# Sums of exponentials by products with ones instead of GpSimd additions, in a fused attention and mixture kernel

## The chip, the cores and the metric

The kernel runs on one core of a Trainium2 chip. The metric is the time of one execution in microseconds (us), measured on the device; several runs are made and the median counts. A core has five engines that run side by side and wait for one another by semaphores: TensorE (PE in the rows; its weight loads are PEld), VectorE (DVE), ScalarE (ACT), GpSimd (POOL) and SyncE (SP), which issues the DMAs.

## What is computed

Three layers, one behind the other. The change is in the first, an attention over pooled queries:

```python
q_pool = q.reshape(B, H, S // 2, 2, D).mean(axis=3)        # B, H, S, D = 4, 8, 1152, 64
scores = np.matmul(q_pool, k.transpose(0, 1, 3, 2)) / np.sqrt(D)
attn = np.exp(scores - scores.max(-1, keepdims=True))
attn = attn / (attn.sum(-1, keepdims=True) + 1e-09)
x = np.matmul(attn, v)                                     # 576 queries a head, 1152 keys
```

Then x (2304 x 512) goes through a soft mixture of eight experts (logits against `phi`, a softmax over the tokens, two products an expert, a softmax over the slots), and its output through a last layer with `w_in` and `w_out` and a piecewise quadratic function between them. `w_in` and `w_out` arrive as 64-bit floats and are turned into 32-bit ones by integer operations on VectorE.

## The kernel before

The attention works on 16 pairs of heads, P = 0 to 15. A pair has nine steps c = 0 to 8 of 128 keys, and each step has two half-steps h (one a head). One loop over g = 9P + c writes the order of all engines by hand. In half-step (c, h) of pair P it puts, in this order:

- `max_half` (line 308): four products into a score tile `mx` for a pair that is 11 steps ahead, whose maximum VectorE takes at line 320 (`mp`). Four such steps give the maxima that are subtracted from the scores later;
- `st` (line 374): eight products into a score tile `st`, and on ScalarE the exponential `e` (line 379), a tile of 128 keys x 576 queries in 32-bit floats;
- `pv` (line 395) of the step before: the products of `e` with the values into `acc[P, i]`, one PSUM bank for each half i of the 576 queries, 288 columns of 512 used;
- whatever `plan` and a table of cast steps have put into the slot (g, h) with `at`.

`mx`, `st` and the small tiles of the tail share a pool of three score tiles. So the products `st` of a half-step need the tile whose maximum VectorE took in the half-step before, or wait for it.

The divisors of the softmax are the sums of `e` over the 1152 keys. In the kernel before, GpSimd adds the nine `e` of each head up (`es_first`, line 389, and `es_add`, line 385); the first addition of the second head is on VectorE, and so are all additions of the last pair. `tail_sum` (line 410, `ts`), in step 10 of the pair, that is step 1 of the next one, sums over the 128 partitions by four products with a column of ones, each into 32 partitions of a score tile, and ScalarE copies the result to `sq` (line 412). The transposes `tr` (line 423), `tx` (434) and `tb` (461) and the division follow in steps 11 to 13.

VectorE has other work in the slots: the cast of `w_out` and `w_in` (lines 190 to 214, tile `wst`, 11 of the 18 half-steps of a pair, from the end of pair 0 to pair 13), `kn` (line 263) and `qn` (286) that prepare keys and queries of a later pair, and `mm` and `qn` (353, 355) that close the maxima. After the maxima of a pair are closed, a DMA transposes `qn` into `q`, which `st` of that pair reads. GpSimd also adds the query pairs (line 276, one instruction a pair).

The attention ends at about 552 us of the span; experts and last layer follow, and the change does not touch them.

Of the kernel before, what the change touches and what calls it, by code (L numbers as in the profile page):

```python
# [33 lines left out]
LQK = 20  # L34
LPT = 6
WPH = 3
ESF = 0, 1
ESE = (lambda n: n.gpsimd, lambda n: n.vector)
REA = 0


@with_exitstack
def fused_kernel(ctx: ExitStack, tc: tile.TileContext, q, k, v, phi, w1, w2, w_in, w_out, out):
    nc = tc.nc
# [12 lines left out]
    LEAD = NK + 2  # L57
# [27 lines left out]
    zcol = cols[0:128, 1:2]  # L85
# [7 lines left out]
    ones = cols[0:128, 10:11]  # L93
# [71 lines left out]
    xT = x_p.tile([128, HPB, TQ], F32, tag="xT", name="xT")  # L165
# [193 lines left out]
    E, Es, acc = {}, {}, {}  # L359

    def acc_tile(i, name):
        return acc_p.tile([128, 512], F32, tag=f"acc{i}", name=name)
# [16 lines left out]
        nc.scalar.activation(out=e, in_=ps[:, :, 0:HQ], func=AF.Exp, scale=ESC)  # L379
        E[P, c, h] = e  # L380

    def es_add(P, c, h):

        eng = nc.vector if P == NP - 1 or h == 1 and NK * P + c >= NP * NK - LEAD else nc.gpsimd
        eng.tensor_tensor(out=Es[P, h], in0=Es[P, h], in1=E[P, c, h], op=ALU.add)  # L385

    def es_first(P, h):
        Es[P, h] = g3.tile([128, 2, HQ], F32, tag=f"es{h}", name=f"es{P}_{h}")
        (nc.vector if P == NP - 1 else ESE[h](nc)).tensor_tensor(out=Es[P, h], in0=E[P, 0, h], in1=E[P, 1, h], op=ALU.add)

    def pv(P, c, i):
        if c == 0:
            acc[P, i] = acc_tile(i, f"acc{P}_{i}")
        for h in range(2):
            nc.tensor.matmul(acc[P, i][h * 64:(h + 1) * 64, 0:HQ], lhsT=vt[P][:, h, c, :], rhs=E[P, c, h][:, i, :],  # L395
                             start=(c == 0), stop=(c == NK - 1))


    xr, ss = {}, {}
# [2 lines left out]
        xr[P] = xT[:, P % HPB, :]  # L402
        nc.scalar.activation(out=xr[P][:, i * HQ:(i + 1) * HQ], in_=acc[P, i][:, 0:HQ], func=AF.Copy)

    def tail_sum(P):
        ps = sc_tile(f"ts{P}")
        for h in range(2):
            for i in range(2):
                j = 2 * h + i
                nc.tensor.matmul(ps[32 * j:32 * j + 32, 0, 0:HQ], lhsT=ones.to_broadcast([128, 32]), rhs=Es[P, h][:, i, :], start=True, stop=True)  # L410
        sq = xT[:, 1, 0:HQ] if P == NP - 1 else Es[P, 0][:, 0, :] if P == NP - 2 else g2.tile([128, HQ], F32, tag="sq", name=f"sq{P}")
        nc.scalar.activation(out=sq, in_=ps[:, 0, 0:HQ], func=AF.Copy)
        xr[P, "s"] = sq

    def tail_fin(P, src):
        ss[P] = g4.tile([TT, 3, 4], F32, tag="ss", name=f"ss{P}")
# [154 lines left out]
        for _ in range(n):  # L571
            nc.tensor.matmul(bt["warm"][0][:, 0:128], lhsT=ident, rhs=ident, start=True, stop=True)

    sched = {}

    def at(g, slot, f, *a):
        sched.setdefault((g, slot), []).append((f, a))

    def plan(P):
        b = NK * P  # L580
        if P > 1:
            at(b - LQK, 0, load_qk, P)
            for h in range(2):
                at(b - 18, h, prep_khi, P, h)
                at(b - 17, h, prep_klo, P, h)
                at(b - 17, h, xpose_k, P, h)
            at(b - 18, 0, prep_qp, P)
            at(b - 16, 0, prep_qhi, P)
            at(b - 16, 0, xpose_q1, P)
            at(b - 15, 0, prep_qlo, P)  # L590
            at(b - 15, 1, dup_q1, P)
        if P > 0:
            at(b - 8, 1, load_v, P)
            at(b - 9 if P > 1 else 1, 1, s2_fill, P)
        for h in range(2):
            at(b + 2, ESF[h], es_first, P, h)
            at(b + 9, h, tail_raw, P, h)
        for c in range(2, NK):
            for h in range(2):
                at(b + c, 1, es_add, P, c, h)  # L600
        at(b + 10, 0, tail_sum, P)
        last = P == NP - 1
        if not last:
            at(b + 11, REA, tail_rec, P)
        for i in range(2):
            at(b + (10 if last else 12), i if last else TXN[i], tail_xn, P, i)
            if last:
                at(b + 12, i, tail_mul, P, i)
        if not last:
            for c, sl, *a in TMUL:  # L610
                at(b + c, sl, tail_mul, P, *a)
        if last:
            at(b + 11, 0, tail_rec, P)
        at(b + 13, 1, tail_xt, P)
        if P % HPB == HPB - 1:
            q_ = P // HPB
            if last:
                at(b + LPT, 1, lg_part, q_)
# [26 lines left out]
    with tc.manual_schedule():  # L645
# [6 lines left out]
        for i in range(2):  # L652
            eng = nc.gpsimd if i else nc.vector
# [39 lines left out]
        for g in range(-LEAD, nsteps + 1):  # L693
            mx = [divmod(g + LEAD, NK)] if not NK <= g + LEAD < 2 * NK else []
            mx += [(1, t) for t in range(NK) if P1G[t] == g]
            P, c = divmod(g, NK)
            for h in range(2):
                for PM, tm in mx:
                    if PM < NP:
                        max_half(PM, tm, h)  # L700
                        if h == 1 and tm == NK - 1:
                            max_fin(PM)
                if 0 <= g < nsteps:
                    st(P, c, h)
                if g >= 1:
                    pv(*divmod(g - 1, NK), h)
                slot(g, h)
            if g >= 27 and g % 9 == WPH and nloaded < NWA:
                w_load()
            for ends, gx, nw, nm in ((nsteps - 24, g0x, NW0, "w0"), (nsteps - 19, g1x, NW1, "w1"), (nsteps - 9, g2x, NW2, "w2"),  # L710
                                    (nsteps, gkx, NWK, "wk")):
                if g == ends:
                    gx.close()
                    pool = wtop.enter_context(tc.tile_pool(name=nm, bufs=1, side="right"))
                    wslot += [pool] * nw
                    for _ in range(nw):
                        w_load()
# [33 lines left out]
        ps = over_slots(sc_tile("sT")[:, 0, :], Prun)  # L751
        n = 4 * NS + 4
# [353 lines left out]
```

## Time and profile before

| what | value |
|---|---|
| median of three runs | 817.34 us (816.13 to 818.74) |
| the profiled execution: its time | 819.79 us |
| the profiled execution: its span, first to last instruction | 818.0 us |
| busy in the span: PE / DVE / ACT / POOL | 89% / 78% / 53% / 58% |
| the chain that ended last, by engine | PE 52%, DVE 36%, DMA 5%, issue 4% |
| its largest line | DVE `mp` L320, 13% |

The busy share of TensorE counts an instruction from its start to its modelled end, and products overlap, so it reads too high: how long a product holds the engine is read from the distance of the starts in the timeline. A group's row gives the busy time, the mean of one in ns, and the idle time ahead of it with the engine that ended it. A row of waits gives the sum, how many, and the longest.

### The profile page before, as it was taken

Reading aid. Unit: us, or ns where it says so; the run is one execution under the profiler, and the core shown is the slowest. Engines: PE = TensorE matmul, PEld = TensorE weight load, DVE = VectorE, ACT = ScalarE, POOL = GpSimd, SP = SyncE. Lnnn points to the kernel's source line nnn. Section 1 sums busy time; section 2 is a strip of 40 time slices with the busy share of each in tenths; the row PEclk is TensorE's granted clock in tenths of the full one; section 3 lists DMA queues with packets and bytes.
Section 4 is the critical chain, followed back from the end, with each engine's and each line's share of the span. In section 5 each row is a group of like instructions: output and inputs, shape, how many; then the busy total and the mean of one; then the engine's idle time right before and its main releaser. Section 6 shows DMA issues by size and latency. Waiting matters only on the chain.

```text
span 818.0 us, 17073 instructions
## 1 busy us (share of the span) xinstructions
PE 731.4 (89%) x6744; PEld 534.7 (65%) x6744; DVE 635.1 (78%) x816; ACT 435.9 (53%) x807; POOL 477.3 (58%) x327
## 2 busy tenths in 40 slices
PE   7888888799787888978879989899999999999998
PEld 6665566566565565655656667563378888888887
DVE  6989999998999998999999886445176787666620
ACT  4345556465564564645646556540166767565530
POOL 7397688775877877667777697100234554434330
PEclk9999999999999999999999999999999999999999
DMA  9967859687797598885978862689990000000000
GB/s 207 224 131 178 195 112 238 196 224 172 196 229 202 171 212 219 212 209 144 225 218 202 195 170 88 208 296 347 392 367 28 27 13 14 26 26 26 26 27 26
DMA packets 144096, 135.37 MB, mean 165 GB/s; under 512 B 80912, under 2 KB 100624, under 8 KB 143632
## 3 DMA queue, kind: packets, MB, share of 16 engines
q1 hardware_dynamic: 144016, 134.28, 60.2%
q8 instruction: 53, 0.87, 0.4%
q14 instruction: 27, 0.22, 0.1%
HBM read 91.29 MB, written 17.30 MB: 133 GB/s over the span
## 4 chain that ended last, share of the span: by engine, by line
PE 52%; DVE 36%; DMA 5%; issue 4%; ACT 1%; SPq 1%; DVEq 0%; ACTq 0%
DVE mp L320 13%; PE st L374 8%; PE po L1009 8%; PE po L1008 8%; PE po L1010 8%; PE acc L395 7%; DVE wst L191 4%; PE mx L308 4%; DVE wst L190 3%; DVE wst L199 3%; DVE wst L196 2%; DVE qn L286 2%; PE h L945 2%; PE h L761 2%; DVE qn L355 2%
## 5 line engine op out<-in xcount | busy, mean ns | idle before, releaser
L385 POOL TENSOR_TENSOR es<-es,e 128x576 f32<-128x576 f32 x208 | 323.0, 1576 | 82.7 <-ACT e L379 71.3
L379 ACT ACTIVATE e<-st 128x576 f32<-128x576 f32 x288 | 187.1, 650 | 192.4 <-PE st L374 185.5
L320 DVE TENSOR_REDUCE mp<-mx 128x1 f32<-128x576 f32 x282 | 209.1, 748 | 29.7 <-PE mx L308 29.2
L395 PE MATMUL acc<-e,vf 128*64 128x288 f32 x1152 | 200.2, 412 | 0.3 <-ACT e L379 0.3
L374 PE MATMUL st<-q,K 128*64 128x288 f16 x1152 | 126.3, 290 | 55.2 <-DVE mp L320 53.0
L308 PE MATMUL mx<-K,q 128*64 128x288 f16 x1152 | 127.7, 294 | 18.9 <-DVE mp L320 15.4
L964 POOL TENSOR_TENSOR glo<-r,ghi 128x1024 fp32r<-128x1024 f32 x34 | 81.7, 2404 | 101.5 <-ACT ghi L963 101.5
L374 PE MATMUL st<-q,S 128*64 128x288 f16 x1152 | 126.8, 289 | 2.6 <-DMA q<-qn 2.6
L374 PEld LDWEIGHTS <-K 128*64 128x64 f16 x1152 | 72.1, 110 | 80.1 <-issue 73.8
L308 PEld LDWEIGHTS <-q 128*64 128x64 f16 x1152 | 70.2, 111 | 78.6 <-issue 43.5
L958 DVE TENSOR_TENSOR r<-cl,r 128x1024 f32<-128x1024 f32 x34 | 81.2, 2388 | 38.6 <-ACT cl L957 38.6
L1008 PE MATMUL po<-whi,ghi 128*128 128x512 f32 (+1 forms) x280 | 107.6, 384 | 0.0
L1009 PE MATMUL po<-wlo,ghi 128*128 128x512 f32 (+1 forms) x280 | 107.6, 384 | 0.0
L1010 PE MATMUL po<-whi,glo 128*128 128x512 f32 (+1 forms) x280 | 107.2, 383 | 0.0
L395 PEld LDWEIGHTS acc<-e,vf 128*64 128x64 f32 x1152 | 85.3, 139 | 3.3 <-ACT e L379 1.5
L374 PEld LDWEIGHTS <-S 128*64 128x64 f16 x1152 | 73.8, 111 | 5.1 <-issue 3.1
L948 ACT ACTIVATE r<-h,cols 128x512 f32<-128x512 f32 x68 | 42.9, 686 | 32.9 <-PE h L945 31.4
L1010 PEld LDWEIGHTS po<-whi,glo 128*128 128x128 f32 x280 | 52.6, 188 | 10.5
L1008 PEld LDWEIGHTS po<-whi,ghi 128*128 128x128 f32 x280 | 52.7, 188 | 9.6
L1009 PEld LDWEIGHTS po<-wlo,ghi 128*128 128x128 f32 x280 | 52.7, 188 | 9.3
L949 DVE TENSOR_SCALAR cl<-h 128x512 f32<-128x512 f32 x68 | 43.7, 686 | 18.1 <-ACT r L948 16.7
L963 ACT ACTIVATE ghi<-r 128x1024 fp32r<-128x1024 f32 x34 | 36.1, 1062 | 19.2 <-DVE r L958 19.1
(191 smaller groups left out, 877.9 us busy)
## 6 DMA issues: line engine op xcount, KB each, us to landing
w<-in_moe_w_dram SPq DMA_DIRECT2D x31, 1024.0 KB, 7.8
vf<-in_v_dram SPq DMA_DIRECT2D x16, 576.0 KB, 5.1
kf<-in_k_dram SPq DMA_DIRECT2D x30, 288.0 KB, 3.8
f<-in_moe_w_out_dram SPq DMA_DIRECT2D x16, 512.0 KB, 4.3
f<-in_moe_w_in_dram SPq DMA_DIRECT2D x16, 512.0 KB, 5.6
qf<-in_q_dram SPq DMA_DIRECT2D x30, 256.0 KB, 4.4
S<-K SPq DMA_DIRECT2D x16, 288.0 KB, 5.8
out_dram<-ob SPq DMA_DIRECT2D x17, 256.0 KB, 2.0
```

What stands on the lines that cost most here:

```text
L308: nc.tensor.matmul(ps[p0:p1, i, 0:HQ], lhsT=q1[P][:, t, p0:p1], rhs=kk[:, j * HQ:(j + 1) * HQ], start=True, stop=True)
L320: nc.vector.tensor_reduce(out=mp[P][:, t, a:a + 1], in_=ps[:, :, 0:HQ], op=ALU.max, axis=AX.XY)
L374: nc.tensor.matmul(ps[c0:c0 + 64, i, 0:HQ], lhsT=kk[:, ci, c0:c0 + 64], rhs=f[:, sl[i]], start=first, stop=not first)
L379: nc.scalar.activation(out=e, in_=ps[:, :, 0:HQ], func=AF.Exp, scale=ESC)
L385: eng.tensor_tensor(out=Es[P, h], in0=Es[P, h], in1=E[P, c, h], op=ALU.add)
L395: nc.tensor.matmul(acc[P, i][h * 64:(h + 1) * 64, 0:HQ], lhsT=vt[P][:, h, c, :], rhs=E[P, c, h][:, i, :], start=(c == 0), stop=(c == NK - 1))
L949: nc.vector.tensor_scalar(out=cl[:, a:b], in0=src, scalar1=-1.0, scalar2=1.0, op0=ALU.max, op1=ALU.min)
L958: nc.vector.tensor_tensor(out=r[:, sl], in0=cl[:, sl], in1=r[:, sl], op=ALU.add)
L964: nc.gpsimd.tensor_tensor(out=glo[n, qd][:, sl], in0=r[:, sl], in1=ghi[n, qd][:, sl].bitcast(F32), op=ALU.subtract)
L1008: nc.tensor.matmul(po, lhsT=ghi[n, qd][:, j, sl], rhs=whi[:, f, cs], start=(f == 0), stop=False)
L1009: nc.tensor.matmul(po, lhsT=ghi[n, qd][:, j, sl], rhs=wlo[:, f, cs], start=False, stop=False)
L1010: nc.tensor.matmul(po, lhsT=glo[n, qd][:, j, sl], rhs=whi[:, f, cs], start=False, stop=(f == 15))
```

## The change

VectorE now adds pairs of steps alone: (0, 1), (2, 3) and (4, 5), six additions a pair of heads, one step after the second `e` (`GRP`; `es_add`, line 387 of the new file). Steps 6, 7 and 8 are not added at all. GpSimd adds nothing. The six groups (three sums and three single `e`) go to TensorE: `es_sum` (line 397 of the new file) multiplies each with the column of ones, for the four combinations j of head and query half, each into 32 partitions. The result is accumulated in the banks of the values behind the 288 columns in use: 192 query columns into `acc[P, 0]`, the other 96 into `acc[P, 1]`. The table `TAT` says where: group 0 in half-step (3, 1), group 1 in (5, 1), groups 2 and 3 in (7, 1), and groups 4 and 5 in (0, 0) of the next pair, each time between `st` and `pv`.

Since the two uses of a bank start at different times, both are started by products of zeros, two a bank, over 480 and 384 columns (in `pv` for c = 0, line 407 of the new file), and the other products only add. `tail_sum` issues no products any more: ScalarE copies the 192 and 96 columns to `sq` in half-steps (0, 0) and (0, 1) of the next pair, right behind `tail_raw`. The score tile `ts` is gone.

```diff
+GRP = ((0, 1), (2, 3), (4, 5), (6,), (7,), (8,))
+TAT = ((3, 1, (0,)), (5, 1, (1,)), (7, 1, (2, 3)), (9, 0, (4, 5)))
...
-        eng = nc.vector if P == NP - 1 or h == 1 and NK * P + c >= NP * NK - LEAD else nc.gpsimd
-        eng.tensor_tensor(out=Es[P, h], in0=Es[P, h], in1=E[P, c, h], op=ALU.add)
...
+    def es_sum(P, ns):
+        for n in ns:
+            for i, (c0, c1) in enumerate(((0, 192), (192, HQ))):
+                for j in range(4):
+                    h = j // 2
+                    src = Es[P, n, h] if len(GRP[n]) > 1 else E[P, GRP[n][0], h]
+                    nc.tensor.matmul(acc[P, i][32 * j:32 * j + 32, HQ:HQ + c1 - c0], lhsT=ones.to_broadcast([128, 32]),
+                                     rhs=src[:, j % 2, c0:c1], start=False, stop=False)
...
+            n = HQ + (192 if i == 0 else HQ - 192)
+            z = ident.bitcast(F16)[:, 0:n // 2].unsqueeze(1).to_broadcast([128, 2, n // 2])
+            for h in range(2):
+                nc.tensor.matmul(acc[P, i][h * 64:(h + 1) * 64, 0:n].rearrange("p (a b) -> p a b", a=2),
+                                 lhsT=zcol.bitcast(F16)[:, 0:1].to_broadcast([128, 64]), rhs=z, start=True, stop=False)
...
-                             start=(c == 0), stop=(c == NK - 1))
+                             start=False, stop=(c == NK - 1))
...
-    def tail_sum(P):
-        ps = sc_tile(f"ts{P}")
...
+        c0, c1 = (0, 192) if i == 0 else (192, HQ)
+        nc.scalar.activation(out=xr[P, "s"][:, c0:c1], in_=acc[P, i][:, HQ:HQ + c1 - c0], func=AF.Copy)
...
-            at(b + 2, ESF[h], es_first, P, h)
+            for n, cs in enumerate(GRP):
+                for c in cs[1:]:
+                    at(b + c + 1, h, es_add, P, n, h, c)
             at(b + 9, h, tail_raw, P, h)
-        for c in range(2, NK):
-            for h in range(2):
-                at(b + c, 1, es_add, P, c, h)
-        at(b + 10, 0, tail_sum, P)
+            at(b + 9, h, tail_sum, P, h)
+        for c, i, ns in TAT:
+            pre[b + c, i] = P, ns
...
+                if (g, h) in pre:
+                    es_sum(*pre[g, h])
```

How the order moves is shown at three places. The first is VectorE in steps 4 and 5 of pair 7, before (`mp` is the maximum, `wst` the cast):

```order
L320 TENSOR_REDUCE mp_3502<-mx_6_0_3817 128x1 [waits PE_49]
L199 SCALAR_TENSOR_TENSOR wst_3645<-f_14_3408,wst_3645 128x512 [waits DVE_49]
L320 TENSOR_REDUCE mp_3502<-mx_6_1_3845 128x1 [waits PE_49]
L214 TENSOR_TENSOR wst_3645<-wst_3645,whi_3841 128x512 [waits Activation_49]
L320 TENSOR_REDUCE mp_3502<-mx_7_0_3877 128x1 [waits PE_49]
L190 TENSOR_SCALAR wst_3896<-f_15_3574 128x512 [waits DMAHW6_49,DMAHW4_49]
L191 TENSOR_SCALAR wst_3896<-wst_3896 128x512 [waits DVE_49]
```

And the same place in the changed kernel (its lines stand one further down):

```order
L321 TENSOR_REDUCE mp_3772<-mx_6_0_4119 128x1 [waits PE_49]
L387 TENSOR_TENSOR es_1_0_4142<-e_2_0_4016,e_3_0_4068 128x576 [waits Activation_49]
L200 SCALAR_TENSOR_TENSOR wst_3946<-f_14_3670,wst_3946 128x512 [waits DVE_49]
L321 TENSOR_REDUCE mp_3772<-mx_6_1_4149 128x1 [waits PE_49]
L387 TENSOR_TENSOR es_1_1_4176<-e_2_1_4047,e_3_1_4096 128x576 [waits Activation_49]
L215 TENSOR_TENSOR wst_3946<-wst_3946,whi_4145 128x512 [waits Activation_49]
L321 TENSOR_REDUCE mp_3772<-mx_7_0_4181 128x1 [waits PE_49]
L191 TENSOR_SCALAR wst_4200<-f_15_3858 128x512 [waits DMAHW6_49,DMAHW4_49]
L192 TENSOR_SCALAR wst_4200<-wst_4200 128x512 [waits DVE_49]
```

An addition stands ahead of the cast step in two half-steps that had the cast alone, and the next maximum stands behind both.

The second place is TensorE in half-step (1, 0) of pair 7, before, where the sums of pair 6 are taken behind the first value products of pair 7:

```order
L395 MATMUL acc_0_3665<-e_0_0_3615,vf_3234 64x288 [waits Activation_49]
L395 MATMUL acc_0_3665<-e_0_1_3638,vf_3234 64x288 [waits Activation_49]
L410 MATMUL ts_3668<-es_0_3264,cols 32x288 [waits PE_49,Pool_49]
L410 MATMUL ts_3668<-es_0_3264,cols 32x288
L410 MATMUL ts_3668<-es_1_3288,cols 32x288 [waits Pool_49]
L410 MATMUL ts_3668<-es_1_3288,cols 32x288
```

In the changed kernel the last two groups of pair 6 stand one step earlier, in half-step (0, 0) of pair 7, ahead of the value products of step 8 (`cols` holds the column of ones; `x2` are two rows that differ in the query half):

```order
L397 MATMUL acc_0_3457<-e_7_0_3788,cols 32x192 x2
L397 MATMUL acc_0_3457<-e_7_1_3816,cols 32x192 x2
L397 MATMUL acc_1_3485<-e_7_0_3788,cols 32x96 x2
L397 MATMUL acc_1_3485<-e_7_1_3816,cols 32x96 x2
L397 MATMUL acc_0_3457<-e_8_0_3851,cols 32x192 x2
L397 MATMUL acc_0_3457<-e_8_1_3875,cols 32x192 [waits Activation_49]
L397 MATMUL acc_0_3457<-e_8_1_3875,cols 32x192
L397 MATMUL acc_1_3485<-e_8_0_3851,cols 32x96 x2
L397 MATMUL acc_1_3485<-e_8_1_3875,cols 32x96 x2
L410 MATMUL acc_0_3457<-e_8_0_3851,vf_2981 64x288
```

Sixteen products stand where there were none, and the value products of the step come behind them.

The third place is TensorE at (1, 0) of pair 7 in the changed kernel, the same place as the second fence shows of before:

```order
L407 LDWEIGHTS cols
L407 MATMUL acc_0_3966<-ident,cols 64x480 [waits Activation_49]
L407 LDWEIGHTS cols
L407 MATMUL acc_0_3966<-ident,cols 64x480
L410 MATMUL acc_0_3966<-e_0_0_3897,vf_3490 64x288
L410 MATMUL acc_0_3966<-e_0_1_3938,vf_3490 64x288 [waits Activation_49]
```

The four products `ts`, with their two waits for GpSimd, are gone, and two products of zeros stand ahead of the value products, behind a wait for ScalarE's copies out of the bank.

## Rows read from the trace of the kernel before

**Rows 1.** Windows: start:end, us, busy of PE, PEld, DVE, ACT, POOL; clock, DMA, GB/s.

```profile
61.47:493.10 431.63, 366.17 (x4194) 256.61 (x4193) 405.13 (x524) 244.15 (x513) 324.29 (x207) 0.99 0.78 197
489.04:513.24 24.20, 24.20 (x295) 17.83 (x291) 15.37 (x20) 15.60 (x35) 18.70 (x15) 1.00 0.29 83
```

**Rows 2.** Waits of the whole span: engine, line, releaser, sum in us, times, longest.

```profile
PE st L374 <- DVE mp L320: 53.0, 57, 2.1
PE mx L308 <- DVE mp L320: 15.4, 23, 1.7
```

**Rows 3.** Groups by line and shape, VectorE, 61.47 to 493.10 us.

```profile
L320 DVE TENSOR_REDUCE mp<-mx 128x1 f32<-128x576 f32 x235 | 174.5, 748 | 15.7 <-PE mx L308 15.2
L191 DVE TENSOR_SCALAR wst<-wst 128x512 f32<-128x512 f32 x31 | 37.2, 1200 | 1.1
...
L389 DVE TENSOR_TENSOR es<-e,e 128x576 f32<-128x576 f32 x13 | 10.7, 823 | 0.0
L353 DVE TENSOR_TENSOR mm<-mp 128x9 f32<-128x9 f32 x13 | 5.2, 396 | 0.4
```

**Rows 4.** Instructions of one line, whole span: min/median/max ns, first and last start.

```profile
L191 DVE TENSOR_SCALAR wst<-wst x32: 426/1511/1558, 46.9 to 475.9; 128x512 f32<-128x512 f32 x32
L353 DVE TENSOR_TENSOR mm<-mp x16: 166/582/1055, 25.8 to 509.4; 128x9 f32<-128x9 f32 x15, 128x3 f32<-128x3 f32 x1
L385 DVE TENSOR_TENSOR es<-es,e x16: 751/759/1882, 511.9 to 541.1; 128x576 f32<-128x576 f32 x16
```

**Rows 5.** Timeline of VectorE and GpSimd at 475 us: start, us, engine, line.

```profile
475.51 3.13 POOL L385 TENSOR_TENSOR es<-es,e 128x576 f32<-128x576 f32 x2
475.86 1.52 DVE L191 TENSOR_SCALAR wst<-wst 128x512 f32<-128x512 f32 x1
...
477.30 0.74 DVE L320 TENSOR_REDUCE mp<-mx 128x1 f32<-128x576 f32 x1
```

**Rows 6.** Timeline of TensorE in two half-steps without a wait.

```profile
67.25 0.41 PE L374 MATMUL st<-q,K 128*64 128x288 f16 x4
...
67.73 0.65 PE L395 MATMUL acc<-e,vf 128*64 128x288 f32 x4
68.22 0.41 PE L308 MATMUL mx<-K,q 128*64 128x288 f16 x4
68.47 0.41 PE L374 MATMUL st<-q,K 128*64 128x288 f16 x4
...
69.54 0.53 PE L434 MATMUL tx<-ident,xT 128*96 128x128 f32 x3
...
70.27 0.41 PE L374 MATMUL st<-q,K 128*64 128x288 f16 x4
```

**Rows 7.** Timeline of TensorE around one call of the old sums.

```profile
60.60 0.94 PE L395 MATMUL acc<-e,vf 128*64 128x288 f32 x4
61.47 0.69 PE L410 MATMUL ts<-es,cols 128*32 128x288 f32 x8
62.09 0.44 PE L308 MATMUL mx<-K,q 128*64 128x288 f16 x4
```

**Rows 8.** Weight loads of the old sums: min/median/max ns.

```profile
L410 PEld LDWEIGHTS ts<-es,cols x128: 105/107/109, 61.5 to 542.3; 128*32 128x32 f32 x128
```

**Rows 9.** Groups of TensorE in 61.47 to 493.10 us: first and last of five for the logits.

```profile
L477 PE MATMUL lp<-xT,phs 128*32 128x288 f32 x48 | 3.5, 412 | 0.0
...
L524 PE MATMUL ln<-ident,xT 32*96 32x32 f32 x18 | 1.4, 210 | 0.9 <-ACT xT L513 0.9
```

**Rows 10.** Timeline of all engines where the last maxima close.

```profile
509.37 1.05 DVE L353 TENSOR_TENSOR mm<-mp 128x9 f32<-128x9 f32 x1
...
510.46 1.36 DVE L355 TENSOR_SCALAR qn<-mm 128x9 f16<-128x9 f32 x1
...
511.84 1.32 SPq L357 DMA_TRANSPOSE q<-qn  x1
...
513.24 0.50 PE L374 MATMUL st<-q,K 128*64 128x288 f16 x4
...
516.35 0.69 PE L374 MATMUL st<-q,S 128*64 128x288 f16 x4 [2.61 <-DMA q<-qn]
```

More of the change, by code (lines that the diff above doesn't have):

```diff
@@ L380, in st, with es_add @@
         E[P, c, h] = e
-    def es_add(P, c, h):
-        eng = nc.vector if P == NP - 1 or h == 1 and NK * P + c >= NP * NK - LEAD else nc.gpsimd
-        eng.tensor_tensor(out=Es[P, h], in0=Es[P, h], in1=E[P, c, h], op=ALU.add)
-    def es_first(P, h):
-        Es[P, h] = g3.tile([128, 2, HQ], F32, tag=f"es{h}", name=f"es{P}_{h}")
-        (nc.vector if P == NP - 1 else ESE[h](nc)).tensor_tensor(out=Es[P, h], in0=E[P, 0, h], in1=E[P, 1, h], op=ALU.add)
+    def es_add(P, n, h, c):
+        a, b = (E[P, GRP[n][0], h], E[P, c, h]) if c == GRP[n][1] else (Es[P, n, h], E[P, c, h])
+        if c == GRP[n][1]:
+            Es[P, n, h] = g3.tile([128, 2, HQ], F32, tag=f"es{h}", name=f"es{P}_{n}_{h}")
+        nc.vector.tensor_tensor(out=Es[P, n, h], in0=a, in1=b, op=ALU.add)
+    def es_sum(P, ns):
[6 more added lines that the diff above has]
+                                     rhs=src[:, j % 2, c0:c1], start=False, stop=False)
     def pv(P, c, i):
@@ L403, in tail_raw, with tail_sum @@
         nc.scalar.activation(out=xr[P][:, i * HQ:(i + 1) * HQ], in_=acc[P, i][:, 0:HQ], func=AF.Copy)
-    def tail_sum(P):
-        ps = sc_tile(f"ts{P}")
-        for h in range(2):
[L408 to L413, printed above, removed]
+    def tail_sum(P, i):
+        if i == 0:
+            last = [Es[x] for x in Es if x[0] == P and x[2] == 0][-1]
+            xr[P, "s"] = xT[:, 1, 0:HQ] if P == NP - 1 else last[:, 0, :] if P == NP - 2 else \
+                g2.tile([128, HQ], F32, tag="sq", name=f"sq{P}")
+        c0, c1 = (0, 192) if i == 0 else (192, HQ)
+        nc.scalar.activation(out=xr[P, "s"][:, c0:c1], in_=acc[P, i][:, HQ:HQ + c1 - c0], func=AF.Copy)
     def tail_fin(P, src):
@@ L572, in warm @@
             nc.tensor.matmul(bt["warm"][0][:, 0:128], lhsT=ident, rhs=ident, start=True, stop=True)
-    sched = {}
+    sched, pre = {}, {}
     def at(g, slot, f, *a):
@@ L595, in plan @@
         for h in range(2):
-            at(b + 2, ESF[h], es_first, P, h)
+            for n, cs in enumerate(GRP):
+                for c in cs[1:]:
+                    at(b + c + 1, h, es_add, P, n, h, c)
             at(b + 9, h, tail_raw, P, h)
-        for c in range(2, NK):
-            for h in range(2):
-                at(b + c, 1, es_add, P, c, h)
-        at(b + 10, 0, tail_sum, P)
+            at(b + 9, h, tail_sum, P, h)
+        for c, i, ns in TAT:
+            pre[b + c, i] = P, ns
         last = P == NP - 1
```

2 lines of the change are left out of this document (removed).

## The prediction

> **What bounds the kernel now.** I read the windows first, then the waits, then VectorE's groups with their minima, then TensorE's timeline. The change acts in the attention alone. Its steady part, 13 pairs from one call of the old sums to the one 13 pairs later, takes 431.63 us, 33.2 us a pair, and VectorE is busy for 405.13 us of it, 94% or 31.2 us a pair [rows 1]. TensorE waits there for VectorE: the products `st` and `mx` waited 53.0 and 15.4 us for the maxima `mp` [rows 2]. In pair 14, where no cast is left, it is the other way round: VectorE is busy for 15.37 of 24.20 us and TensorE for all of it [rows 1]. So a steady pair is bound by VectorE in many half-steps and by TensorE in the others.
>
> Why is VectorE so full? Its maxima take 748 ns [rows 3] and do not vary. The rest does: the clamp of line 191 takes 426 ns at least and 1511 at the median, the nine-element `mm` 166 and 582 [rows 4]. At 475.86 us the clamp starts while a GpSimd addition is running and takes 1.52 us [rows 5]; the additions that VectorE makes itself take 751 to 759 ns, but up to 1882 in the places where GpSimd is still adding [rows 4]. I read the excess as waiting for GpSimd's additions.
>
> The Trainium skill ("SBUF — State Buffer", Who interferes with whom) states such a lock: VectorE instructions with two SBUF inputs, or in a two-port mode, and GpSimd instructions block each other for a whole instruction, and a reduction never takes part. This trace agrees, with the steady 748 ns of `mp` against the 426 to 1558 ns of the clamp.
>
> **VectorE, part by part.** Removed excess: for ten groups of the steady part (lines 190, 191, 193, 196, 199, 214, 263, 286, 353, 355), count times mean less the free duration, the minimum or for 286 its 758 ns without GpSimd at work. The first is 31 x (1200 - 426) = 24.0 us and the last 13 x (396 - 166) = 3.0 us [rows 3, 4]; all ten give 111 us, 8.6 us a pair. Added: six sums at 759 ns [rows 4] are 4.55 us a pair, less the 10.7/13 = 0.8 us of the old one [rows 3]: 3.7. VectorE falls from 31.2 to 26.3 us a pair. GpSimd keeps one addition a pair (line 276), which may still block one instruction; I allow 0.3 us.
>
> **TensorE, part by part.** An unhindered half-step takes 1.22 us, from `st` at 67.25 to `st` at 68.47, and with three transposes 1.80 [rows 6]. A pair has 18 of them, three sets of three transposes (0.58 each) and one of six (0.8, an estimate from these), and the old sums: from 61.47 to the next product 0.62 us, and some 0.1 ahead of it [rows 7]. That is 21.96 + 1.74 + 0.8 + 0.7 = 25.2 us. Pair 14 bears it out: five of its half-steps lack `mx` (0.24 to 0.25 us each, from 68.22 to 68.47 [rows 6]), so 24.0 by this price against 24.2.
>
> The new sums: the old call streams 288 columns in four tiles of 32, and holds the engine for 0.62 us, of which 0.48 would be its columns if the four tiles run at once (the value products, with two tiles at once, take 0.49 from 67.73 to 68.22 [rows 6]). The remaining 0.14, and 0.1 on the way in, I read as the price of changing from 64 to 32 columns and back. A group now streams 192 + 96 = 288 columns, 0.48 us; six are 2.9 us, four calls add 4 x 0.2 = 0.8. The zeros are 480 and 384 columns of 16-bit products, at 0.12 us for 288 (a quarter of the 0.49 of `st` [rows 6]) 0.36 us. Less 0.7 for `ts`, TensorE rises by 3.3 to 28.5 us a pair.
>
> A rule speaks against the change here: the Trainium skill ("TensorEngine Tiling (Array Packing)", Key Properties) says that a change of the tiling mode drains TensorE, and the change makes eight a pair out of two. The page gives no figure. The trace agrees, with 0.62 us from the sums to the next product; were switching free, the sum below would be 0.8 x 13, some 10 us, lower.
>
> **How the two meet.** With three score tiles, `st` waits for the maximum of the half-step before, so neither engine can run far ahead. I price each half-step by the larger of TensorE's products and VectorE's work of the slot before. VectorE's instructions start some 0.07 us before the one ahead ends (475.86 + 1.52 against 477.30 [rows 5]), so each counts that much less: a maximum 0.70, a cast step 1.18 now and 0.58 free, a sum 0.70. Before, VectorE is the larger in twelve half-steps, by 0.66 us behind each of eight lone casts, 1.6 where `kn` stands with a cast, 0.6, 0.3 and 0.3 in three more: 25.2 + 8.1 = 33.3 us. The trace has 33.2, of which the five groups for the logits (3.5 to 1.4 us, 13.5 together [rows 9]) are 1.0: 32.2. So the rule overstates by 1.1, since short lags are caught up. After, VectorE is the larger by 0.75 us in (4, 1) and (6, 0), where a sum stands with a cast, by 0.6 behind `kn`, 0.55 behind the first sum with the two small steps of the division, 0.45 where the maxima close, and 0.3 in all in the lone casts; the slot (4, 0) is hidden by the six transposes, and the slots of TensorE's own calls are hidden as well: 28.5 + 3.4 = 31.9. The overstatement taken off whole leaves 30.8, and as its share of VectorE's excess (1.1 of 8.1, here 0.5) 31.4; I take 31.1 between them. The gain is 1.1 us a pair, and 13 pairs give -14.3.
>
> The added waits: TensorE's sums wait for VectorE's additions, behind which the rest of the half-step is queued, but each sum stands a step later than its addition, and the maximum that stands behind the addition has been waited for by then: nothing. The zeros wait for ScalarE's two copies out of the bank, a step earlier: nothing, covered by `mx` and `st`; uncovered, 0.3 us a pair. An exponential of step 6 or 7 reuses a tile that an addition reads; it is a step late at the earliest: nothing.
>
> **The ends.** The first pair has few casts, so it pays the sums and gets little: +0.5. Pair 14 is TensorE's: +3.3. At its end `mm` and `qn` take 1.05 + 1.36 us, and the transposed `q` is waited for, 2.61 us, with slower products behind it (0.69 instead of 0.41) [rows 10, 6]. Free, these two take some 0.35, and two groups of sums (1.1, counted above) stand in the gap, so the wait goes, with some 0.8 of the slow products: -3.4. The last pair has its own sums, +3.3, and the last call, in place of `ts`, +0.5. Together +4.2 us. What follows the attention stays.
>
> **The sum.** -14.3 + 4.2 = -10.1. The profiled execution took 819.79 us, 1.8 more than its span, and would take 809.7; the median of the runs is 2.5 lower, 817.34, and the forecast 807 us.
>
> **The rivals.** *No change*, 817 us: the lags are not caught up in the changed kernel, because sums, casts and transposes stand closer together. Then a pair takes 31.9, 13 x 0.3 = 4 are gained and the ends cost 4.2. For it: two slots with a sum and a cast, one behind another. Against: the price of before needs such catching up to come out.
> *TensorE's pace*, 773 us: VectorE at 26.3 of 31 us catches up everywhere, a pair takes 28.5, and 13 x 3.7 = 48 are gained less 4.2. Against: 15.4 us of waits are for `mx`, which lags cannot reach in a kernel with slack.
> *Slower*, 826 us: the 96-column calls. A pass over 96 columns lasts 0.08 us, and two such passes a tile need a second weight load of 107 ns [rows 8] that hides behind 0.24 us today. Unhidden it costs up to 0.2 us a call; 96 calls, nearly all in half-steps that TensorE bounds, are up to +19 on 807, and the verdict turns slower (above 819.8) from 0.13 a call on. For it: no row shows such short passes with weights this size. Against: in `ts` eight loads and products go through in 0.62 us.
> *It does not do what it says*, 860 us: VectorE's excess is not GpSimd's. Then VectorE has 3.7 us a pair more and TensorE 3.3, which cost some 3 a pair where the two meet, 39 and the ends' 4. Against: rows 4 and 5.
>
> **How the numbers follow.** What a measurement can tell from no change is about 0.3%, 2.5 us: 814.9 to 819.8. The forecast, 0.64, by itself spans 798 to 815; no change 0.14; TensorE's pace, or half of it, 0.06; the short passes 0.13; the wrong cause 0.03. Faster is the first and third, 0.70; same 0.14; slower 0.16. The range is 793 to 822: it leaves out most of TensorE's pace and the worse half of the two slower cases.
>
> **What would show it.** The clamp's median near 0.43 us, the additions near 0.76 and GpSimd busy for some 130 us prove VectorE's part; a call of one group at 0.62 us up to the next product, and two at 1.1, TensorE's. The same 13 pairs should take about 32.1 us each, logits among it, with VectorE near 82% busy and most waits of `st` for `mp` in (4, 1) to (6, 1). The forecast is wrong if a 96-column call takes over 0.3 us, if the additions take well over 0.76, or if `st` no longer waits for `mp` at all.

## The result and the profile after

The changed kernel takes **808.56 us** (median of four runs, 807.59 to 808.96) against 818.04 us of the kernel before (four runs), a ratio of 0.988 with an interval of 0.984 to 0.991. In a later set of runs, with more of both, it was 807.73 against 819.74 us, 0.986 [0.983, 0.988]. The forecast was 807.

The page of the changed kernel, the profiled execution of 807.59 us: its span, the busy time of each engine, the chain that ended last, and VectorE's maxima (its lines stand one further down, so `mp` is line 321):

```profile
span 805.4 us, 19576 instructions
...
PE 781.2 (97%) x8216; PEld 562.7 (70%) x8216; DVE 558.8 (69%) x879; ACT 434.0 (54%) x823; POOL 130.4 (16%) x104
...
PE 80%; DVE 9%; ACT 4%; DMA 4%; issue 2%; SPq 1%; ACTq 0%; DVEq 0%
...
L321 DVE TENSOR_REDUCE mp<-mx 128x1 f32<-128x576 f32 x282 | 211.2, 751 | 78.7 <-PE mx L309 77.9
```

The maxima last as long as before, and VectorE now stands idle ahead of them, for TensorE. TensorE is now 80% of the chain that ended last and VectorE 9%; before it was 52% and 36%. The waits have turned round with it (sum, times, longest):

```profile
PE mx L309 <- DVE mp L321: 5.4, 11, 0.8
...
PE st L375 <- DVE mp L321: 2.5, 6, 0.8
```

Before, these two were 15.4 and 53.0 us [rows 2].

The windows from the first `st` of pair 1 to that of pair 14, then pair 14 and the last pair (columns as in [rows 1]):

```profile
58.45:473.03 414.58, 406.12 (x5385) 279.37 (x5381) 341.62 (x590) 243.41 (x528) 19.34 (x13) 1.00 0.80 205
473.03:501.25 28.22, 28.15 (x388) 19.85 (x383) 14.91 (x24) 15.75 (x36) 0.00 (x0) 1.00 0.34 81
501.25:527.05 25.80, 25.51 (x333) 16.29 (x331) 4.51 (x8) 15.24 (x36) 0.00 (x0) 1.00 0.69 246
```

Thirteen pairs take 414.6 instead of 431.9 us (the same stretch of before, st to st), 31.9 a pair. VectorE is busy for 341.62 us of them, 26.3 a pair or 82%. Pair 14 takes 28.2 instead of 24.2 us. In the last pair the wait for the transposed `q` [rows 10] is gone.

Four of VectorE's lines (minimum, median, maximum in ns, as in [rows 4]): the clamp, `mm`, `qn` and the sums.

```profile
L192 DVE TENSOR_SCALAR wst<-wst x32: 426/427/430, 51.4 to 461.1; 128x512 f32<-128x512 f32 x32
...
L354 DVE TENSOR_TENSOR mm<-mp x16: 164/170/173, 26.7 to 496.2; 128x9 f32<-128x9 f32 x15, 128x3 f32<-128x3 f32 x1
...
L356 DVE TENSOR_SCALAR qn<-mm x16: 186/188/190, 26.9 to 496.4; 128x9 f16<-128x9 f32 x16
...
L387 DVE TENSOR_TENSOR es<-e,e x96: 689/748/757, 38.9 to 520.0; 128x576 f32<-128x576 f32 x96
```

The clamp's median fell from 1511 to 427 ns and that of `mm` from 582 to 170 ns, within 4 ns of the minima that the trace of before had shown.

TensorE's timeline shows the price of a call (start, us, engine, line): first value products with transposes behind them and no call, then a call of one group, both in pair 6, then a half-step without a call, a call of two groups and the zeros:

```profile
228.33 0.68 PE L410 MATMUL acc<-e,vf 128*64 128x288 f32 x4
228.94 0.53 PE L447 MATMUL tx<-ident,xT 128*96 128x128 f32 x3
...
229.91 0.41 PE L375 MATMUL st<-q,S 128*64 128x288 f16 x4
230.26 0.70 PE L397 MATMUL acc<-es,cols 128*32 128x192 f32 x16
230.88 0.71 PE L410 MATMUL acc<-e,vf 128*64 128x288 f32 x4
231.52 0.53 PE L447 MATMUL tx<-ident,xT 128*96 128x128 f32 x3
...
232.50 0.41 PE L375 MATMUL st<-q,S 128*64 128x288 f16 x4
232.74 0.65 PE L410 MATMUL acc<-e,vf 128*64 128x288 f32 x4
233.27 0.44 PE L309 MATMUL mx<-K,q 128*64 128x288 f16 x4
233.65 0.44 PE L375 MATMUL st<-q,K 128*64 128x288 f16 x4
...
501.49 0.42 PE L375 MATMUL st<-q,S 128*64 128x288 f16 x4
501.84 1.19 PE L397 MATMUL acc<-e,cols 128*32 128x192 f32 x32
502.95 0.71 PE L410 MATMUL acc<-e,vf 128*64 128x288 f32 x4
503.49 0.41 PE L375 MATMUL st<-q,K 128*64 128x288 f16 x4
...
504.96 0.37 PE L407 MATMUL acc<-ident,cols 128*64 128x480 f16 x2
505.16 0.66 PE L410 MATMUL acc<-e,vf 128*64 128x288 f32 x4
```

From the sums to the next product it is 0.62 us for one group and 1.11 for two. But the call also starts 0.35 us behind the start of the last four products of `st`, where the value products start 0.24 behind. And the value products behind a call hold the engine a little longer: 0.64 us up to the transposes, where those without a call take 0.61 (228.33 to 228.94), and 0.54 up to the next `st` (502.95 to 503.49), where 0.49 is usual [rows 6]. The zeros take 0.20 us.

Both engines meet in the distance from the `st` of one half-step to the next. These are its medians over the ten pairs of 1 to 13 without logits, taken from TensorE's timelines (an unhindered half-step is 1.22, [rows 6]):

```
half-step   0,0  0,1  1,0  1,1  2,0  2,1  3,0  3,1  4,0  4,1  5,0  5,1  6,0  6,1  7,0  7,1  8,0  8,1
before     1.80 1.22 2.03 2.29 1.83 1.22 1.80 1.85 1.81 2.01 1.33 1.70 1.54 1.55 2.41 1.89 1.22 1.22
after      2.49 1.22 1.42 1.59 1.83 1.46 1.83 2.58 1.40 2.01 1.40 2.02 1.22 1.46 1.42 2.51 1.22 1.22
```

The calls stand out in (3, 1), (5, 1), (7, 1) and (0, 0), the old one at (1, 0) is gone, and so is most of VectorE's excess in (1, 1), (4, 0) and (7, 0).

Five half-steps stay at 1.40 to 1.46 us: (2, 1), (4, 0), (5, 0), (6, 1) and (7, 0). Most of these wait for ScalarE, although the profile lists hardly a wait of `st` for it (two, 0.7 us). In pair 2, from the sum of (6, 0) to the `st` of (7, 0):

```profile
112.34 0.75 DVE L387 TENSOR_TENSOR es<-e,e 128x576 f32<-128x576 f32 x1
...
112.67 0.41 PE L375 MATMUL st<-q,K 128*64 128x288 f16 x4
...
113.00 0.69 DVE L197 SCALAR_TENSOR_TENSOR wst<-f,wst 128x512 int32<-128x512 int32 x1
...
113.43 0.65 ACT L380 ACTIVATE e<-st 128x576 f32<-128x576 f32 x1 [0.56 <-PE st L375]
113.61 0.75 DVE L321 TENSOR_REDUCE mp<-mx 128x1 f32<-128x576 f32 x1
...
114.13 0.44 PE L375 MATMUL st<-q,K 128*64 128x288 f16 x4
```

The sum and the cast step hold the maximum up, and it runs until 114.36 us. The `st` of (7, 0) starts at 114.13, so it does not wait for that maximum. It starts 0.05 us behind the end of the exponential of (6, 1), 113.43 + 0.65, and in the order of the program it waits for ScalarE there: it is given the score tile of the `st` of (6, 1). Had it waited for the maximum, it would have started at least 0.23 us later.

Counted over the ten pairs without logits, 66 half-steps are more than 0.06 us longer than TensorE's own work, by 1.9 us a pair in all. In 46 of them the next `st` starts within 0.08 us of the end of such an exponential (1.0 us a pair), in 14 of the end of a maximum (0.5 us); what holds the other six up (0.3 us) is not shown. In the kernel before it was a maximum in 63 of 92 (5.7 of 6.9 us a pair). So what is said of the score tiles ahead of the prediction, that `st` needs the tile of the maximum of the half-step before, holds for most of the long half-steps of the kernel before, and for few of those that are left.

### The profile page after: what moved, and what is told of

It is laid out like the page before. It is cut to its first block, busy times and chain, and to the rows that moved or that the text cites. A ratio compares the mean times of both kernels' runs of the same rounds, so it can differ in the third digit from the quotient of the medians.

```text
span 805.4 us, 19576 instructions
## 1 busy us (share of the span) xinstructions
PE 781.2 (97%) x8216; PEld 562.7 (70%) x8216; DVE 558.8 (69%) x879; ACT 434.0 (54%) x823; POOL 130.4 (16%) x104
## 4 chain that ended last, share of the span: by engine, by line
PE 80%; DVE 9%; ACT 4%; DMA 4%; issue 2%; SPq 1%; ACTq 0%; DVEq 0%
PE st L375 16%; PE acc L410 14%; PE po L1025 8%; PE po L1024 8%; PE po L1026 8%; PE mx L309 7%; PE acc L397 7%; DVE mp L321 4%; ACT e L380 3%; PE h L961 2%; PE tx L447 2%; PE h L777 2%; DMA q<-qn 1%; PE s2o L829 1%; PE tb L474 1%
## 5 line engine op out<-in xcount | busy, mean ns | idle before, releaser
L410 PE MATMUL acc<-e,vf 128*64 128x288 f32 x1152 | 195.3, 412 | 0.6 <-ACT e L380 0.6
L309 PE MATMUL mx<-K,q 128*64 128x288 f16 x1152 | 124.4, 296 | 8.6 <-DVE mp L321 5.4
L375 PE MATMUL st<-q,K 128*64 128x288 f16 x1152 | 121.9, 288 | 6.0 <-DVE mp L321 2.5
L375 PE MATMUL st<-q,S 128*64 128x288 f16 x1152 | 121.9, 286 | 0.4 <-DMA q<-qn 0.4
L309 PEld LDWEIGHTS <-q 128*64 128x64 f16 x1152 | 64.7, 111 | 68.7 <-issue 22.2
L375 PEld LDWEIGHTS <-K 128*64 128x64 f16 x1152 | 68.1, 109 | 28.4 <-issue 19.2
L277 POOL TENSOR_TENSOR qf<-qf 128x576 f32<-128x576 f32 x14 | 20.8, 1483 | 402.9 <-DMA qf<-in_q_dram 282.4
L410 PEld LDWEIGHTS acc<-e,vf 128*64 128x64 f32 x1152 | 75.9, 136 | 13.2 <-ACT e L380 1.8
L387 DVE TENSOR_TENSOR es<-e,e 128x576 f32<-128x576 f32 x96 | 70.7, 739 | 7.8 <-PE acc L397 7.8
L375 PEld LDWEIGHTS <-S 128*64 128x64 f16 x1152 | 69.8, 110 | 3.3 <-issue 0.6
```

Source lines behind the costliest of these rows:

```text
L309: nc.tensor.matmul(ps[p0:p1, i, 0:HQ], lhsT=q1[P][:, t, p0:p1], rhs=kk[:, j * HQ:(j + 1) * HQ], start=True, stop=True)
L375: nc.tensor.matmul(ps[c0:c0 + 64, i, 0:HQ], lhsT=kk[:, ci, c0:c0 + 64], rhs=f[:, sl[i]], start=first, stop=not first)
L387: nc.vector.tensor_tensor(out=Es[P, n, h], in0=a, in1=b, op=ALU.add)
```

## The experiments

**Theory**: GpSimd's additions held VectorE up. Without them VectorE needs 26 us a pair, and the time goes to where TensorE's new products put it. **Rivals**: GpSimd was not the cause, and something else in the new order made VectorE faster; TensorE's products with ones are covered and VectorE's sums are what is left to pay; the price of a call is its switching.

**GpSimd adds again.** The changed kernel, with GpSimd adding the nine `e` of pairs 0 to 12 as before, into a tile that nobody reads.

```diff
+    def es_old(P, c, h):
...
+        nc.gpsimd.tensor_tensor(out=old[P, h], in0=old[P, h], in1=E[P, c, h], op=ALU.add)
...
+        if P < NP - 3:
+            for h in range(2):
+                for c in range(1, NK):
+                    at(b + max(c, 2), h if c == 1 else 1, es_old, P, c, h)
```

> The changed kernel, and GpSimd again adds the exponentials of pairs 0 to 12 (16 additions a pair) into a tile that nobody reads. No sum is waited for; only the blocking of VectorE comes back. Theory (the gain is VectorE freed from GpSimd's additions): the clamp of the cast goes back from 0.43 to a median of 1.2 us or more, VectorE's own six sums to some 1.2 us, VectorE to 26.3 + 8.6 + 6 x 0.5 = 38 us a pair, which then sets the pace: 13 pairs x (38 - 31) = 90 us slower than the changed kernel, about 900 us, slower than before too. Rival (the gain is from the tail: no sum tile, no wait for GpSimd's result): 808 to 812 us, and the clamp stays at 0.43 us.

It took 896.35 us (893.28 to 898.76), 1.094 [1.089, 1.099] of the kernel before and 88 us more than the changed one. Of this kernel the clamp, the sums, a wait, and the window of the same 13 pairs:

```profile
L192 DVE TENSOR_SCALAR wst<-wst x32: 427/1510/1678, 55.1 to 550.6; 128x512 f32<-128x512 f32 x32
...
L387 DVE TENSOR_TENSOR es<-e,e x96: 690/1257/1969, 38.4 to 609.5; 128x576 f32<-128x576 f32 x96
```

```profile
PE st L375 <- DVE mp L321: 47.1, 51, 2.4
```

```profile
65.80:562.54 496.74, 424.54 (x5385) 290.01 (x5381) 463.43 (x590) 244.37 (x528) 330.30 (x207) 0.98 0.66 170
562.54:590.76 28.22, 28.15 (x387) 19.85 (x383) 14.91 (x24) 15.73 (x36) 0.00 (x0) 1.00 0.34 81
```

No engine waits for the sums of these additions; ScalarE waits 9.3 us in nine places to write an exponential into a tile that they read, a small part of the 88. The additions bring the clamp back from 427 to 1510 ns and put (463.43 - 341.62)/13 = 9.4 us a pair on VectorE. Pair 14, where GpSimd adds nothing, takes its 28.22 us as before the edit. So the excess is GpSimd's, and the rival falls.

**The kernel before without GpSimd's additions of steps 2 to 8.**

```diff
-        eng.tensor_tensor(out=Es[P, h], in0=Es[P, h], in1=E[P, c, h], op=ALU.add)
+        if eng is nc.vector:
+            eng.tensor_tensor(out=Es[P, h], in0=Es[P, h], in1=E[P, c, h], op=ALU.add)
```

> The kernel before, without GpSimd's additions of steps 2 to 8 (208 of them): the divisors miss these steps. TensorE and VectorE have the instructions of before. Theory (GpSimd blocks VectorE): VectorE falls by 8.6 to 22.6 us a pair, TensorE's 25.2 us set the pace with some 1.5 of VectorE's excess on top, 27 to 28 us a pair instead of 33.2 with logits at 1.0: 13 x 5 = 65 us faster, and 5 at the ends, about 748 us. Rival (VectorE's long instructions have another cause, a DMA or its own operands): 815 to 818 us.

It took 756.15 us (753.61 to 759.06), 0.923 [0.918, 0.927]. The window of its 13 pairs:

```profile
53.86:428.89 375.03, 354.01 (x4190) 251.77 (x4187) 316.54 (x525) 242.57 (x515) 41.96 (x26) 1.00 0.91 227
```

56.9 us less than before in 13 pairs, 4.4 a pair, for some 7 us a pair less of VectorE's time (316.54 against 405.13 us [rows 1]): from there on, as I read it, TensorE sets the pace. This is what the additions cost in these pairs, and about all that could be won. (The first addition of a pair is left on GpSimd, and some of the excess with it: VectorE is busy for 24.3 us a pair, where 31.2 less the whole excess of 8.6 would be 22.6.)

**The changed kernel without the products with ones** in pairs 0 to 14; the zeros stay, and so do VectorE's sums.

```diff
-                if (g, h) in pre:
+                if (g, h) in pre and pre[g, h][0] == NP - 1:
```

> The changed kernel without the products with ones for pairs 0 to 14: the divisors of these are only the zeros. VectorE's six sums and ScalarE's copies stay. Theory (after the change TensorE sets the pace, its four calls lie on the path with their 3.6 us a pair): half-steps (3,1), (5,1), (7,1) and (0,0) shrink by 0.7, 0.7, 1.2 and 1.2 us less what VectorE then takes there, some 0.8 in all: 3.0 x 15 = 45 us faster than the changed kernel, about 763 us. Rival (VectorE still sets the pace): under 10 us faster, about 800 us.

It took 759.12 us (756.26 to 762.51), 0.927 [0.922, 0.931]. Its 13 pairs:

```profile
54.50:430.86 376.36, 360.45 (x4138) 260.37 (x4134) 343.52 (x590) 242.17 (x528) 20.65 (x13) 1.00 0.91 226
```

38.2 us of the 13 pairs of the changed kernel are these products, 2.9 a pair. VectorE is as busy as in the changed kernel, so nearly the whole new price lies on TensorE.

**The changed kernel without VectorE's sums** in pairs 0 to 13; the products with ones read one `e` of each group in their place.

```diff
-            for n, cs in enumerate(GRP):
+            for n, cs in enumerate(GRP if P > NP - 3 else ()):
...
-                    src = Es[P, n, h] if len(GRP[n]) > 1 else E[P, GRP[n][0], h]
+                    src = Es[P, n, h] if (P, n, h) in Es else E[P, GRP[n][-1], h]
```

> The changed kernel without VectorE's six sums in pairs 0 to 13: the products read the second exponential of each pair of steps, so the divisors miss steps 0, 2 and 4. TensorE's products are the same. Theory (TensorE sets the pace and VectorE's six sums, 4.2 us a pair, are hidden but for an excess of some 1.2 us a pair in the half-steps with a sum and a cast): 0.9 x 14 = 12 us faster than the changed kernel, about 796 us. Rival (VectorE sets the pace): up to 4.2 x 14 = 59 us faster, about 750 us.

It took 799.94 us (798.94 to 800.11), 0.976 [0.971, 0.981]. Its 13 pairs:

```profile
58.12:465.55 407.43, 398.80 (x5386) 277.27 (x5382) 298.00 (x512) 244.09 (x528) 19.04 (x13) 1.00 0.83 209
```

Some 44 us of VectorE's work are worth 7.2 us (8.7 against the changed kernel's second profile, below): 0.55 to 0.67 us a pair for six sums. The half-steps (2, 1), (5, 0), (6, 1) and (7, 0), 1.40 to 1.46 us in the changed kernel, are back at 1.22: this is where the sums show, by 0.2 us each. Without the sums these `st` are given other score tiles: that of (7, 0) in pair 2 waits for VectorE in the order of this program, and not for the exponential ahead of it. So the 0.2 us belong to VectorE's sums, and in the changed kernel most of them are waited out behind ScalarE; why the tiles go round in another order is not shown. (4, 0) takes 1.46 us here too, so its excess is not the sums'.

**The changed kernel, again**, beside the three that follow.

> The changed kernel once more, for the comparison with the three kernels beside it on one chip. Every theory: 808 us within 3 us, and 13 steady pairs at 31.9 us each with logits.

807.73 us (807.35 to 808.78), and 416.08 us for the 13 pairs, 1.5 more than in its first profile. So differences of 1 to 2 us in this window are not read as effects.

**Four pairs of steps instead of three.** Steps 6 and 7 are added by VectorE in (8, 0) and (8, 1), each beside a cast step, and one group of products falls away in (7, 1).

```diff
-GRP = ((0, 1), (2, 3), (4, 5), (6,), (7,), (8,))
-TAT = ((3, 1, (0,)), (5, 1, (1,)), (7, 1, (2, 3)), (9, 0, (4, 5)))
+GRP = ((0, 1), (2, 3), (4, 5), (6, 7), (8,))
+TAT = ((3, 1, (0,)), (5, 1, (1,)), (7, 1, (2,)), (9, 0, (3, 4)))
```

> Steps 6 and 7 are added by VectorE too, in (8,0) and (8,1), so TensorE sums five groups instead of six. Theory (TensorE sets the pace; a group costs it 0.49 us, and a sum that stands with a cast costs 0.2 us of the path): the half-step of (7,1) shrinks from 2.51 to 2.02 us, the last half-step of the pair grows by 0.2, the first stays: 0.3 x 15 = 4 us faster than the changed kernel, 804 us. Rival (VectorE sets the pace, the larger of the two in full): 0.5 us less and 0.76 more a pair, 812 us.

806.93 us (804.98 to 807.57), 1 us less than the changed kernel's 807.73, between the 804 of the theory and the 812 of the rival. The half-step (7, 1) fell from 2.51 to 2.02 us, as priced, but (8, 1) rose from 1.22 to 1.46 and (0, 0) from 2.49 to 2.69. I read this as the call in (0, 0) waiting for the sum that VectorE makes in (8, 1), right ahead of it. The next kernel tests that.

**The same with one sum earlier**: the sum of steps 6 and 7 stands in (7, 1) for the first head, and in (8, 1) for the second as before.

```diff
-                    at(b + c + 1, h, es_add, P, n, h, c)
+                    at(*((b + c + h, 1) if n == 3 else (b + c + 1, h)), es_add, P, n, h, c)
```

> As the five groups before, with the two new sums in (7,1) and (8,1): in (7,1) no cast stands, and behind (8,1) TensorE's own call covers VectorE. Theory (what a sum costs depends on what stands with it): 0.49 us less a pair and at most 0.1 more, 6 us faster than the changed kernel, 802 us. Rival (VectorE's whole work counts, wherever it stands): the same as with the sums in (8,0) and (8,1).

**802.06 us** (801.39 to 803.39), 0.979 [0.976, 0.981] of the kernel before, and better than both. Its 13 pairs:

```profile
56.87:467.75 410.88, 400.74 (x5177) 274.95 (x5174) 359.88 (x617) 243.11 (x528) 19.67 (x13) 1.00 0.80 207
```

Now (7, 1) is 2.02, (8, 1) 1.22 and (0, 0) 2.49 us: the gain of the group is kept, 0.4 us a pair, and 1.2 us of additional work a pair on VectorE cost next to nothing. My reading of the kernel ahead of it holds in the traces of both: there the sum made in (8, 1) ends 0.6 to 1.1 us behind the `st` of (0, 0) in nine of the pairs 2 to 14, and the value products behind the call come up to 0.54 us later (one pair set aside, in which the whole call starts late); here it ends 0.61 us behind it at the latest, and they come at most 0.07 us later. But the place of that sum is the same in both. What made it late was the sum of (8, 0) with its cast step ahead of it, not its own place.

**Three calls instead of four.** Groups 2 to 5 all in (0, 0).

```diff
-TAT = ((3, 1, (0,)), (5, 1, (1,)), (7, 1, (2, 3)), (9, 0, (4, 5)))
+TAT = ((3, 1, (0,)), (5, 1, (1,)), (9, 0, (3, 2, 4, 5)))
```

> Six groups in three calls instead of four: the groups of (7,1) go to the call in (0,0) of the next pair. The products are the same. Theory (each call pays some 0.25 us for changing from 64 to 32 columns and back): 0.25 x 16 = 4 us faster than the changed kernel, 804 us. Rival (the change of columns costs nothing by itself, and the longer call is only moved): 808 us; should the exponential of (0,0), which now waits for the sums that read its tile, hold up the pair, slower than that.

809.98 us (808.21 to 812.65), 2 us more than the changed kernel, not 4 less. (7, 1) fell from 2.51 to 1.42 us, (0, 0) rose from 2.49 to 3.49: a call less gives back 0.09 us a pair there, and the 13 pairs take 416.67 us, no less than 416.08. A fixed price is there (a call of one group costs its half-step 0.78 to 0.80 us, one of two 1.27 to 1.29, one of four 3.49 - 1.22 = 2.27, so 0.49 a group and 0.3 a call), but (7, 1) did not come down to 1.22. And the long call lets ScalarE wait, a row that the changed kernel has not:

```profile
ACT e L380 <- PE acc L397: 24.9, 16, 3.4
```

The code says why. The exponentials of four half-steps in six go round in four tiles, so that of (0, 0) is written into the tile of (6, 0). Group 3, which is step 6, is read in (7, 1) in the changed kernel, but here in (0, 0), behind `st`: ScalarE waits for those products, 1.6 us each time. The forecast of 804 counted the switching alone. And (7, 1) ends 0.05 us behind an exponential, as (7, 0) does: the 0.2 us that it kept are such a wait, and not TensorE's own work. So what a call less is worth by itself was not cleanly measured.

## Why the prediction came out

The sign was right, and so was what it rests on: VectorE freed from GpSimd's additions, and TensorE's products as the new price. How the two engines meet was priced by a wait that the changed kernel hardly has. That the time came out so near, 807 forecast and 808.56 measured, is in part luck, since errors of both signs cancel. By its steps:

**VectorE** came out as priced: 26.3 us a pair and 82% busy, both as forecast, the clamp at 427 ns (forecast 0.43 us), the sums at 748 (forecast 759), GpSimd busy for 130 us in the whole span. Reading the minima of a line as its free duration [rows 4] was sound: with GpSimd nearly quiet, the medians of the clamp, `mm` and `qn` fell to their minima. That the cause is GpSimd was read from one overlap [rows 5]; the first experiment shows it.

**TensorE's products** were priced too low. The part inside a call was right (0.62 and 1.11 us to the next product, forecast 0.62 and 1.1), and so were the zeros (0.20 + 0.17 us, forecast 0.36). By half-steps the four calls cost 0.78 + 0.80 + 1.29 + 1.27 = 4.14 us a pair, not 3.7. The term that was too small is the fixed price of a call: 0.3 us, where the prediction read 0.14 + 0.1 from the old call and then added only 0.2. Some 0.05 of the rest are the value products *behind* a call, which [rows 7] does not show, since `mx` stood behind the old one. The old call was worth 0.77 us ((1, 0) takes 1.99 in the kernel before without GpSimd's additions), not 0.7. So TensorE rose by 4.14 + 0.37 - 0.77 = 3.7 us a pair, not 3.3.

**How the two meet** was priced too high, and this hides the other error. I add TensorE's own work up from the table: 18 x 1.22, the calls and zeros, three transposes' excess of 0.6 three times, one of 0.79, that is 21.96 + 4.14 + 0.37 + 1.8 + 0.79 = 29.1 us. A pair without logits took 30.9 (the mean of ten), so the excess over it is 1.9 us, where 2.6 were forecast (31.1 - 28.5). The step that failed is the premise that `st` waits for the maximum of the half-step before, and with it the larger-of rule: 0.75 us for a sum beside a cast, 0.6 behind `kn`, 0.55 behind the first sum, 0.45 where the maxima close. In the table these are some 0.2 each, in (5, 0) and (6, 1), (1, 1), (2, 1) and (7, 0). Most of the longer half-steps wait for the exponential just before, and so a late maximum costs only what this chain from `st` over `e` to the next `st` takes beyond 1.22 us. The overstatement should have been taken off whole, as the price of before had asked for, and more.

Together a pair gained (431.9 - 414.6)/13 = 1.3 us instead of 1.1, 13 pairs 17.3 instead of 14.3 (by the changed kernel's second profile 15.8, 1.2 a pair).

**The ends**: pair 14 cost 4.0 (forecast 3.3; by the prices above it is 3.7). The last pair came to -0.7 (forecast 3.3 - 3.4 = -0.1): the wait for `q` is gone, with `mm` and `qn` at 0.17 and 0.19 us. The last call cost nothing that shows (278.4 us from the last `st` to the end against 278.3; forecast 0.5). **The first pair was misread**: 26.3 us instead of 28.1, a gain of 1.8 where I forecast a loss of 0.5. I wrote that it has few casts, but the row of the clamp says that they begin at 46.9 us [rows 4], ten microseconds ahead of the end of that pair, and GpSimd adds in all of it; without these additions the pair takes 22.9 us in the kernel before. From the first `st` on, the sum is -17.3 - 1.8 + 4.0 - 0.7 + 0.1 = -15.7 us.

**What the sum did not have**: the profiled spans differ by 12.6 us, not 15.7, since the first `st` starts at 32.19 us instead of 29.04, behind instructions that the change leaves alone. In the eight other profiles it starts at 30.7 to 32.5 us, in the one with the code of before at 30.97, so 29.04 was early. Windows of 10 to 20 and 20 to 33 us, the kernel before and then the changed one:

```profile
10.00:20.00 10.00, 6.65 (x63) 4.83 (x63) 7.58 (x16) 5.35 (x9) 6.62 (x5) 0.83 0.96 209
20.00:33.00 13.00, 9.56 (x101) 7.09 (x101) 12.29 (x24) 3.33 (x7) 0.71 (x1) 1.00 0.85 180
```

```profile
10.00:20.00 10.00, 6.26 (x50) 4.63 (x52) 7.02 (x15) 5.06 (x9) 7.45 (x5) 0.66 1.08 230
20.00:33.00 13.00, 10.11 (x77) 7.74 (x78) 10.75 (x22) 1.01 (x3) 0.32 (x1) 0.74 0.74 157
```

TensorE's mean granted clock is 1.00 (2.4 GHz throughout) in the second window of before, and 0.74 in that of the changed kernel, where a part ran at 1.2 GHz. What sets this from run to run, and how much of it is in the medians, whose difference is 9.5 us, stays open. So the attention gained more than the 10.1 us that were forecast, and the late start took some of it back, which no step of the prediction has.

**The rivals.** *Slower*, by the short passes: a second group adds 0.49 us for 288 columns, so no weight load shows there. *TensorE's pace*: TensorE's own work is 29.1 us a pair, not 28.5, and some 1.9 of waits stay on top, so 773 was out of reach. But this rival was near in one thing, that VectorE's work is nearly all hidden: without any of its sums the 13 pairs took only 7 to 9 us less. *It does not do what it says*: excluded by the first two experiments. *No change*: the lags are there, but cost some 0.2 us each, not their whole length.

**The indicators.** All but one held. The waits of `st` for `mp` in (4, 1) to (6, 1) are missing: the whole span has six waits for `mp`, 2.5 us, which is near the sign of being wrong that the prediction names, that `st` no longer waits for `mp` at all. It is the sign of the premise above. The waits that are there, 1.40 to 1.46 us in the table, are mostly not listed: as I read it, they are shorter than the tail of a product that is still modelled as busy. In the timeline above, `mx` starts at 233.27 and lasts 0.44 us, to 233.71; the next `st` starts at 233.65, 0.38 behind `mx` where 0.25 is usual [rows 6], and no wait is given. An exponential ended there 0.05 us ahead, the maximum 0.43.

Of the Trainium skill ("TensorEngine Tiling (Array Packing)", Key Properties), the rule that a change of the tiling mode drains the engine agrees with the fixed 0.3 us a call. In the kernel with three calls two of the eight changes were gone and nothing came back in the time, for the wait that it added.

## What to carry to other kernels

Where VectorE is full and GpSimd is at work beside it, compare the minimum of each of VectorE's lines with its mean: count times the difference was what GpSimd cost it here (8.6 us a pair by this count, 9.4 when the additions were put back), and an experiment that takes GpSimd's work out, or puts it back for nobody, tests it in one run. What is won is only the distance to the next engine (here 7 us a pair off VectorE were worth 4.4), and moving the work to that engine spends most of it: of the 57 us that GpSimd's additions cost the 13 pairs, 38 went to the products with ones, and the cheapest further step was to give VectorE a little of it back. Price a step of TensorE from `st` to `st`, with what stands behind it, and not by its own length. And where engines share a few tiles, look up for each wait which engine ended last: the tile that is waited for can change with the order of the program.

## What the runs showed of the hardware

- A VectorE instruction of nine elements a partition has no protection by being short: `mm` fell from 582 to 170 ns at the median, and in the kernel before took up to 1055 ns [rows 4]. With the additions put back for nobody its median is 581 ns. I read this as waiting for a GpSimd addition of some 1.6 us to end [rows 5].
- Four tiles of 32 columns do run at once for 32-bit products: by the records of the trace, eight products over 192 columns and eight over 96 held TensorE for 0.49 us more, as much as four over 288 with two tiles at once (0.49 us, [rows 6]).
- A call with tiles of 32 columns between products with tiles of 64 cost a fixed 0.3 us beside its columns: some 0.1 ahead of its first product, 0.14 within, and 0.05 in the products behind.
- A sum of 0.75 us on VectorE cost the pair 0.1 us on average here (0.55 to 0.67 for six), since TensorE then waited for ScalarE's exponential of the half-step before (0.05 us behind its end) and not for the late maximum. A sum that the next call needs cost more where another sum and two cast steps stood close ahead of it ((0, 0) at 2.69 us instead of 2.49).
